# Seven block products instead of eight in the first feed-forward layer of the last four chunks

## The chip, the cores and the metric

The kernel runs on one core of a Trainium2 chip. The metric is the device time of one execution in microseconds. Engines are called as in the profile: PE (TensorE, matrix products), PEld (its weight loads), DVE (VectorE), ACT (ScalarE), POOL (GpSimd) and SP (the queue that issues DMAs).

## What is computed

Attention over 8 batches and 8 heads (512 local rows with a window of 32, 32 global rows), then per batch of 544 rows and 512 columns a Fourier mixing and a feed-forward block:

```python
x = attn_out.transpose(0, 2, 1, 3).reshape(8, 544, 512)
u = x + real(fft(fft(x, axis=1), axis=2))
un = (u - mean(u)) / sqrt(var(u) + 1e-6)            # per row
out = u + relu(un @ w_ch1) @ w_ch2                   # w_ch1 512 x 2048, w_ch2 2048 x 512
```

The change is in `un @ w_ch1` alone.

## The kernel before

Every operand of a matrix product is split into two float16 parts (hi and lo), and a product is three matmuls: hi·hi, hi·lo, lo·hi, summed in PSUM.

The rows go through the feed-forward block in 17 **chunks** of 256 rows. Chunks 2b and 2b+1 are rows of batch b, chunk 16 holds the 32 rows that each batch has left over. For a chunk, `l_bn` and `l_v` make mean and variance, `l_un` normalizes, `l_hi` (ACT) and `l_lo` (DVE) split, `l_turn` turns the result by a DMA transpose into the tile `uh`. Then there are 8 steps `fp`: `f_first` (L1047, 24 matmuls of 256 columns) makes 256 of the 2048 hidden columns for the 256 rows, `f_hi` (ACT, L1052) and `f_lo` (DVE, L1056) take relu and split, `f_second` (L1066, 12 matmuls of 512 columns) adds their share of the second layer to two accumulators in PSUM. `f_end` (L1071) scales and adds u, `f_out` (L1077, L1080) stores.

The order of work is made when the program is built. `Plan` is a list scheduler: each job has an engine, an estimated duration, dependencies, buffer rings and a target `t`; on every engine the ready job with the lowest target goes next. Jobs of the same function keep the order in which they were added (`j.prev`), so `f_end` of one chunk never goes behind that of a later chunk. What the scheduler decides is each engine's order. Its times are not kept on the chip: a `hold` delays a job in the plan, but on the chip the instruction runs as soon as what it waits for is done. Attention and the mixing (`d_...` functions) have low targets, the feed-forward matmuls have 10000 added to theirs, so they fill what PE has free. `targets` works targets backwards from successors that have one, and a job added with `back=False` gives none to those before it.

On PE, the attention of the last batch ends at about 821 us of the profile, its mixing at about 850 us, chunk 12 at about 855 us, and the rest is chunks 13 to 16, 42 us each.

POOL has the `lo` halves of attention, some sums of the mixing, and `l_root` (a few tiny instructions per chunk).

Of the kernel before, what the change touches and what calls it, by code (L numbers as in the profile page):

```python
# [14 lines left out]
AF = mybir.ActivationFunctionType  # L15
ALU = mybir.AluOpType
# [26 lines left out]
PEM, PEM0, SPM = 1.5, 0.6, 0.2  # L43
# [34 lines left out]
def shape_constants():  # L78
    a = np.arange
    t = 127 - a(P)[:, None]  # L80
    r = a(P)[:, None]
    k = np.concatenate([a(128, 0, -1), a(144, 272), [0], a(129, 144), [272], a(129, 144)])
    k = np.concatenate([k[0::2], k[1::2]])[None, :]
    tt = np.concatenate([[0], a(129, 144), [272], a(415, 400, -1)])[:, None]
    c1 = np.zeros((P, 2, 2, NK), np.float16)
    c1t = np.zeros((P, 2, NK), np.float16)
    c2 = np.zeros((P, 2, 2, 2, NH), np.float16)
    for i, fn in enumerate((np.cos, np.sin)):
        for j, v in enumerate(_hi_lo(fn(2 * np.pi * ((t + 1) * k % T) / T))):
# [24 lines left out]
class Job:
# [180 lines left out]
class Kern:  # L295
    def __init__(self, tc, stack, ins, out):
        self.tc, self.nc, self.out = tc, tc.nc, out
        nc = self.nc
        self.qk, self.vd, self.gd = ins["qk"], ins["v"], ins["g"]
        self.wd = (ins["moe_w_ch1"], ins["moe_w_ch2"])  # L300
        ep = lambda **k: stack.enter_context(tc.tile_pool(**k))
        c = self.cp = ep(name="cst", bufs=1)
        self.mskb = c.tile([P, 4, 256], U16, name="msk")
        self.msk = self.mskb.bitcast(BF16)
        self.consts = ins
        self.part = c.tile([P, P], F32, name="part")
# [4 lines left out]
        vN = c.tile([P, 2, 1300], F16, name="vN")  # L311
# [3 lines left out]
        self.vf = [c.tile([P, 5, 2, D], F32, name=f"vf{i}") for i in range(4)]  # L315
# [658 lines left out]

    def u_all(self, c):
        if c == 16:
            return self.u[16]
        return self.X[c // 2][:, (slice(1, 4, 2) if c % 2 else slice(0, 3, 2))]

    def u_row(self, c, j):  # L980
        return self.u_all(c)[:, j]

    def l_load(self):
        self.u[16] = u = self.p3.tile([P, 4, DM], F32, name="X")[:, 0:2]
        for j in range(2):
            self.nc.sync.dma_start(u[:, j], self.ul[j])

# [289 lines left out]
    def jobs_chunk(self, add, c):  # L1277
# [112 lines left out]
```

## Time and profile before

| | us |
|---|---|
| median of 3 runs | 1030.37 (1029.78 to 1032.76) |
| the profiled execution: its time | 1033.84 |
| its span, first to last instruction | 1032.1 |
| PE busy in the span | 929.6 (90%) |
| DVE, ACT, POOL busy | 658.1, 589.4, 531.8 |

The span is shorter than the execution's own time by 1.7 us, which lie around it. The profiled execution was 3.5 us slower than the median of the runs. Busy time counts overlapping matmuls once and does not say whether PE runs at its peak; for that one reads the distance between the starts of successive groups.

### The profile page before, as it was taken

The numbers are of one execution on the slowest core, as the hardware profiler recorded it, in microseconds if no ns is written. First come the engines' busy times: TensorE is split into PE (matmuls) and PEld (weight loads), VectorE is DVE, ScalarE is ACT, GpSimd is POOL, SyncE is SP. The second block draws the span as 40 slices with busy tenths as digits, with TensorE's granted clock in tenths as the row PEclk, the third lists the DMA queues.
The fourth block names the chain that finished last, engine by engine and source line by source line (L and its number), as shares of the span: only waits on it lengthen the run. The fifth ranks groups of instructions, "written<-read, shape, count | busy, mean of one in ns | idle before, by whom it ended". The sixth has DMA issues, their size and how long they took to land. (4 is left out here: it accounts for less than half of the span.)

```text
span 1032.1 us, 25192 instructions
## 1 busy us (share of the span) xinstructions
PE 929.6 (90%) x9864; PEld 651.0 (63%) x9864; DVE 658.1 (64%) x1773; ACT 589.4 (57%) x1291; POOL 531.8 (52%) x797
## 2 busy tenths in 40 slices
PE   2354459999999999999999999999999999999996
PEld 1243347767677767676766676777767676666673
DVE  4887999977768855785598568856775456311111
ACT  7996769973677477637863876487436332111110
POOL 7999756862687278626863774486437302000000
PEclk9985569999999999999999999999999999999998
DMA  9898356462685287328752864466225402102000
GB/s 364 254 269 238 105 107 138 106 140 42 141 130 133 45 160 154 77 55 147 134 131 53 132 155 96 88 117 140 39 55 102 83 1 64 42 1 41 2 21 21
DMA packets 221359, 111.52 MB, mean 108 GB/s; under 512 B 196376, under 2 KB 203704, under 8 KB 221240
## 3 DMA queue, kind: packets, MB, share of 16 engines
q1 hardware_dynamic: 221240, 109.91, 48.5%
q8 instruction: 77, 1.26, 0.5%
q14 instruction: 42, 0.34, 0.1%
HBM read 47.37 MB, written 9.44 MB: 55 GB/s over the span
## 5 line engine op out<-in xcount | busy, mean ns | idle before, releaser
L1047 PE MATMUL ps<-uh,wh 128*128 128x256 f16 x3264 | 379.7, 274 | 0.9 <-DMA uh<-unh 0.9
L1066 PE MATMUL acc<-wh,h 128*128 128x512 f16 x1632 | 375.2, 380 | 1.5 <-DVE h L1056 1.0
L1047 PEld LDWEIGHTS <-wh 128*128 128x128 f16 x3264 | 316.1, 98 | 51.2 <-issue 2.0
L1066 PEld LDWEIGHTS <-h 128*128 128x128 f16 x1632 | 154.3, 98 | 170.3 <-issue 2.5
L1056 DVE SCALAR_TENSOR_TENSOR h<-ps,h 128x512 f16<-128x512 f32 x136 | 93.6, 689 | 236.2 <-ACT h L1052 236.0
L1052 ACT ACTIVATE h<-ps 128x512 f16<-128x512 f32 x136 | 80.7, 593 | 256.4 <-PE ps L1047 255.8
L628 POOL TENSOR_TENSOR ph<-pe,ph 128x448 f16<-128x448 f32 (+1 forms) x128 | 139.4, 1103 | 79.3 <-ACT ph L623 63.3
L612 DVE CUSTOM_DVE_ANT_0 pe<-bk,msk,z 128x224 f32<-128x224 f32 (+1 forms) x256 | 102.4, 454 | 17.4 <-PE bk L604 14.2
L619 ACT ACTIVATE pe<-pe,nm 128x224 f32<-128x224 f32 (+1 forms) x256 | 104.7, 476 | 14.2 <-DVE nm L612 13.9
L1027 POOL TENSOR_TENSOR ve<-ve 128x2 f32<-128x2 f32 x17 | 3.9, 230 | 179.8 <-DVE un L1007 179.8
L649 PE MATMUL bk<-vN,pl 128*128 128x65 f16 x768 | 67.4, 201 | 26.6 <-DMA pl<-ph 17.9
L623 ACT ACTIVATE ph<-pe 128x448 f16<-128x448 f32 (+1 forms) x128 | 71.0, 579 | 22.0 <-DMA pl<-ph 15.2
L649 PEld LDWEIGHTS <-pl 128*128 128x128 f16 x768 | 59.5, 103 | 28.8 <-DMA pl<-ph 23.5
L652 PEld LDWEIGHTS <-pl 96*128 96x128 f16 (+1 forms) x768 | 57.5, 103 | 10.0 <-issue 5.9
L604 PE MATMUL bk<-kT,qT 64*128 64x192 f16 (+2 forms) x1536 | 57.5, 221 | 6.5 <-POOL kT L588 4.2
L604 PEld LDWEIGHTS <-qT 64*128 64x128 f16 x1536 | 50.1, 99 | 20.8 <-issue 16.7
L652 PE MATMUL bk<-vB,pl 96*128 96x65 f16 (+1 forms) x576 | 51.5, 202 | 0.0
L563 POOL TENSOR_TENSOR vN<-vf,vN 128x640 f16<-128x640 f32 x32 | 45.8, 1431 | 6.8 <-ACT vN L559 6.6
L419 PE MATMUL wl<-wm,partb 128*128 128x256 bf16 x64 | 18.8, 398 | 32.0 <-DVE wm L409 32.0
L588 POOL TENSOR_TENSOR kT<-qk,kT 128x559 f16<-128x559 f32 x32 | 40.7, 1271 | 11.8 <-ACT kT L583 11.6
L573 ACT ACTIVATE qk<-qk,z 128x559 f32<-128x559 f32 x64 | 43.7, 729 | 2.1 <-DVE z L514 2.0
L508 ACT ACTIVATE junk<-qk 128x512 f16<-128x512 f32 x64 | 41.3, 645 | 4.4 <-DMA qk<-in_qk 3.4
(170 smaller groups left out, 1350.0 us busy)
## 6 DMA issues: line engine op xcount, KB each, us to landing
qk<-in_qk SPq DMA_DIRECT2D x32, 535.5 KB, 5.2
rw<-in_moe_w_ch SPq DMA_DIRECT2D x22, 512.0 KB, 5.2
vf<-in_v SPq DMA_DIRECT2D x32, 320.0 KB, 3.3
out<-X SPq DMA_DIRECT2D x16, 512.0 KB, 3.1
raw<-in_moe_w_ch SPq DMA_DIRECT2D x10, 512.0 KB
vB<-vN SPq DMA_DIRECT2D x32, 97.5 KB, 2.2
vB<-vN SPq DMA_DIRECT2D x64, 32.5 KB, 2.0
pl<-ph SPq DMA_TRANSPOSE x128, 3.2
```

The costliest lines, as they stand in the source:

```text
L563: self.nc.gpsimd.tensor_sub(vN[:, :, 1, :, 0:64], self.st[p]["vf"], vN[:, :, 0, :, 0:64])
L604: nc.tensor.matmul(S[h][:, t + w0:t + w1], qT[r, a, j], kT[r, k0:k0 + w1 - w0], start=m == 0, stop=m == 2)
L612: nc.vector.tensor_tensor_reduce(self.per[j][:, h, 0:w], S[h][:, t:t + w], self.msk[:, j, 0:w], z[:, 8:9], 3e38, op0=ALU.add, op1=ALU.min, ...
L619: self.nc.scalar.activation(pe[:, h], pe[:, h], AF.Exp, bias=nm[:, h:h + 1], scale=-1.0)
L623: self.nc.scalar.activation(ph[:, 0, :, 0:WIDE[i % 4]], self.per[i % 4][:, :, 0:WIDE[i % 4]], AF.Copy)
L628: self.nc.gpsimd.tensor_sub(ph[:, 1, :, 0:w], self.per[i % 4][:, :, 0:w], ph[:, 0, :, 0:w])
L649: nc.tensor.matmul(pv[:, j % 2, h], pl[:, 4 * a + 2 * h], vN[:, j, c, h, :], start=m == 0, stop=False)
L652: nc.tensor.matmul(pv[:, j % 2, h], pl[0:n, 4 * a + 2 * h + 1], vb, start=False, stop=m == 2)
L1047: nc.tensor.matmul(ps[:, q], wt[:, w, c0:c0 + P], uh[:, :, 4 * a + kt, :], start=n == 0, stop=n == 11)
L1052: self.nc.scalar.activation(h[:, 0], self.fps[c, fp], AF.Relu)
L1056: self.nc.vector.scalar_tensor_tensor(h[:, 1], self.fps.pop((c, fp)), 0.0, h[:, 0], op0=ALU.max, op1=ALU.subtract)
L1066: nc.tensor.matmul(self.acc_f[c][j], h[:, a, q, j * P:(j + 1) * P], self.w[1, f][:, w, :], start=f == 0 and a == 0 and w == 0, stop=f == 1 ...
```

## The change

The last four chunks are done in two **pairs**, (13, 14) and (15, 16). For a pair the first layer is a product of 2 x 2 blocks: two halves of the 512 input columns, two chunks of rows, and for each `s` (0 to 7) two blocks of 128 hidden columns. It is done by Strassen's scheme in Winograd's form, with 7 block products P1 to P7 (each 6 matmuls of 256 columns: 2 for the block's 256 inputs, times 3 for hi and lo) instead of 8.

- **Sums of weights** (`t_sum`, `t_mix`, `t_lo` on POOL, `t_hi` on ACT), 8 times: two sums of hi and lo (512 columns each), four differences of 256, two splits. They lie in buffers of attention and start when its last results are there (`late`).
- **Sums of rows**: `s_pre` normalizes chunk A of a pair for P1 and P2; `s_un` normalizes both chunks, `s_mix` (4 DVE instructions of 256) makes the sums, `s_hi`, `s_lo`, `s_turn` split and turn four kinds of blocks (g = 0 to 3) for each of two row halves j. The split results go through a ring of two buffers (`unh`).
- **Phase one** of a pair: for each s, P1 and P2; their sum is relu'd, split and given to the second layer of chunk A (6 matmuls of 512 columns, `p_second` n = 0).
- **Phase two**: for each s, P4, P5, P6, P7, P3, seven small copies and sums (`p_copy` on ACT, `p_sum` on DVE), two splits, and the rest of the second layer: n = 2 (both blocks of chunk B, 12 matmuls), then n = 1 (chunk A, 6 matmuls).
- The mixing of the last batch gets its targets 40 us earlier (`BOOST`); `l_bn`, `l_v` of the four chunks give no targets backwards any more. `vf` and `pe`, four tiles each, become slices of one tile each.

```diff
+PAIRS = ((13, 14), (15, 16))
+PL = 45.0
+T_AT, T_PACE = 826.0, 7.5
+BOOST = 40.0
+PROD = {"P1": (0, 0, 0), "P2": (0, 2, 2), "P3": (2, 2, 3), "P4": (3, 0, 7), "P5": (1, 0, 4), "P6": (1, 2, 5), "P7": (2, 0, 6)}
...
+    def t_sum(self, n, o):
...
+        self.nc.gpsimd.tensor_add(f.rearrange("p a c -> p (a c)"), w[:, 0], w[:, 1])
+    def t_mix(self, n):
...
+        ve.tensor_sub(a[:, 0], f[:, 1], f[:, 0])
+        ve.tensor_sub(b[:, 0], g[:, 1], f[:, 1])
+        ve.tensor_sub(a[:, 1], g[:, 1], a[:, 0])
+        ve.tensor_sub(b[:, 1], a[:, 1], g[:, 0])
+    def t_hi(self, n):
...
+            self.nc.scalar.activation(t[:, 0, 2 * i:2 * i + 2], v, AF.Copy)
+    def t_lo(self, n):
...
+            self.nc.gpsimd.tensor_sub(t[:, 1, 2 * i:2 * i + 2], v, t[:, 0, 2 * i:2 * i + 2])
...
+    def s_mix(self, u, j):
...
+        ve.tensor_add(s[:, 0], b[:, 0], b[:, 1])
+        ve.tensor_sub(t[:, 0], a[:, 0], b[:, 0])
+        ve.tensor_sub(s[:, 1], s[:, 0], a[:, 0])
+        ve.tensor_sub(t[:, 1], a[:, 1], s[:, 1])
...
+    def p_mul(self, u, s, n):
...
+            for x, y in ((0, 0), (0, 1), (1, 0)):
+                nc.tensor.matmul(ps, w[x], a[:, :, k * y + o + kt, :], start=m == 0, stop=m == 5)
+                m += 1
...
+    def p_sum(self, u, s, o, a, b):
...
+        (ve.tensor_sub if o == "c21" else ve.tensor_add)(v[o], a, v[b])
+    def p_rest(self, u, s, n):
...
+        self.nc.vector.scalar_tensor_tensor(h[:, 1, q], v, 0.0, h[:, 0, q], op0=ALU.max, op1=ALU.subtract)
...
+    def jobs_mixes(self, add):
+        late = [("xM", 31), ("xgo", 7, 1)]
...
+                add("POOL", 1.16, self.t_sum, n, o, r=[self.whobj[0, 4 * (kt + 2 * o) + c], *late], w=[("qT", "T", n, o)], t=T, hold=T)
+            add("POOL", 2.6, self.t_mix, n, r=[("qT", "T", n, 0), ("qT", "T", n, 1)], w=[tw], t=T + 3)
+            add("ACT", 1.1, self.t_hi, n, r=[tw, *done.get(n, [])], w=[home], t=T + 5)
+            add("POOL", 2.4, self.t_lo, n, r=[tw, home], w=[home], t=T + 7)
+    def jobs_duo(self, add, u):
...
+        first = [*end, ("ht", 7), ("uh", 12)] if u == 0 else []
...
+                add("DVE", .58, self.s_un, u, j, n, r=[("uj", c, j), ("ve", c), *first], w=[un[n]], k=[("X", c // 2)], t=L, back=False)
...
+        for s in range(8):
+            b = prod(s, "P1", t)
+            b = prod(s, "P2", t)
+            summ(s, "c11", "P2", "x1", [b, x1, *end], [c11], own)
+            split(s, 0, .36, [c11], [], ("h", "s", u, s, 0), [f], t + STEP / 2 + 1)
+        for s in range(8):
...
+            b = prod(s, "P6", t)
+            summ(s, "x1", "P6", "x1", [b, x1], [x1], xk)
+            b = prod(s, "P7", t)
+            summ(s, "u3", "P7", "x1", [b, x1], [u3, ("xu", u, s)], xk)
+            summ(s, "c12", "x1", "c22", [x1, cz], [c12], [R, *xk], .34)
+            b = prod(s, "P3", t)
+            summ(s, "c21", "u3", "c21", [u3, cw], [cw], [R, ("xu", u, s)], .34)
+            summ(s, "c22", "u3", "c22", [u3, cz], [cz], [R, ("xu", u, s)], .34)
+            split(s, 2, .58, [cw, cz], [R], ("pl", "s", u, s), [f, f + 2], t + 1.5 * STEP + 2)
+            summ(s, "c12", "P3", "c12", [b, c12], [c12], [R])
+            split(s, 1, .36, [c12], [R], ("h", "s", u, s, 1), [f + 2], t + 1.5 * STEP + 1)
+        for n, c in enumerate(PAIRS[u]):
+            for j in range(2):
+                add("DVE", .72, self.f_end, c, j, r=[accs[n][j], ("ve", c), ("uj", c, j)], w=[("uj", c, j)], k=[("X", c // 2)], t=-1e3, back=False)
+            add("SP", .39, self.f_out, c, r=[("uj", c, 0), ("uj", c, 1)], w=[("out", c)], k=[("X", c // 2)], svc=3.2, t=T, back=False)
...
         for c in range(17):
-            self.jobs_chunk(add, c)
+            if c not in MATE:
+                self.jobs_chunk(add, c)
+        self.jobs_mixes(add)
+        for u in range(len(PAIRS)):
+            self.jobs_duo(add, u)
         plan.targets(1.3)
+        for j in plan.jobs:
+            if j.fn.__name__.startswith("d") and j.a[0] == B - 1:
+                j.t -= BOOST
```

## Rows read from the trace of the kernel before

**Rows 1.** The page: busy share of PE and the granted clock of PE in 40 equal slices of the span (tenths).

```profile
PE   2354459999999999999999999999999999999996
PEclk9985569999999999999999999999999999999998
```

**Rows 2.** Waits of PE between 150 us and the end: the longest in total: who waited for whom, total us, times, longest us.

```profile
PE bk L649 <- DMA pl<-ph: 4.2, 4, 2.6
```

**Rows 3.** The first-layer matmuls between 855 and 1023 us: count, busy us and mean ns, idle us before them.

```profile
L1047 PE MATMUL ps<-uh,wh 128*128 128x256 f16 x768 | 88.4, 273 | 0.0
```

**Rows 4.** Timeline of the tail of the kernel, steady part: start us, duration us, engine, line, operation.

```profile
993.46 2.78 PE L1047 MATMUL ps<-uh,wh 128*128 128x256 f16 x24
996.08 2.75 PE L1066 MATMUL acc<-wh,h 128*128 128x512 f16 x12
996.28 0.60 ACT L1052 ACTIVATE h<-ps 128x512 f16<-128x512 f32 x1 [4.61 <-PE ps L1047]
996.91 0.69 DVE L1056 SCALAR_TENSOR_TENSOR h<-ps,h 128x512 f16<-128x512 f32 x1 [4.52 <-ACT h L1052]
998.67 2.78 PE L1047 MATMUL ps<-uh,wh 128*128 128x256 f16 x24
```

**Rows 5.** Timeline of the last matmuls and the end of the kernel.

```profile
1016.92 5.34 PE L1066 MATMUL acc<-wh,h 128*128 128x512 f16 x24
...
1021.09 0.75 DVE L1071 SCALAR_TENSOR_TENSOR X<-acc,ve,X 128x512 f32<-128x512 f32 x1 [2.64 <-PE acc L1066]
1021.87 1.82 SPq L1080 DMA_DIRECT2D out<-X  x2
1022.30 0.75 DVE L1071 SCALAR_TENSOR_TENSOR X<-acc,ve,X 128x512 f32<-128x512 f32 x1 [0.47 <-PE acc L1066]
```

**Rows 6.** Timeline around the end of the last batch's mixing and of chunk 12.

```profile
831.97 0.75 DVE L847 SCALAR_TENSOR_TENSOR eh<-s,dsc,eh 128x512 f16<-128x512 f32 x1
...
836.76 0.35 PE L893 MATMUL bk<-c1r,eh 128*128 128x144 f16 x3
...
849.40 1.65 DVE L945 SCALAR_TENSOR_TENSOR X<-bk,dsc,X 128x256 f32<-128x256 f32 x4
...
850.19 5.35 PE L1066 MATMUL acc<-wh,h 128*128 128x512 f16 x24
...
853.30 0.55 DVE L1007 TENSOR_SCALAR un<-X,ve 128x512 f32<-128x512 f32 x1
...
855.33 1.40 DVE L1071 SCALAR_TENSOR_TENSOR X<-acc,ve,X 128x512 f32<-128x512 f32 x2
855.38 5.40 PE L1047 MATMUL ps<-uh,wh 128*128 128x256 f16 x48
```

**Rows 7.** DMA issues between 800 and 900 us: count and median us from issue to landing.

```profile
uh<-unh SPq DMA_TRANSPOSE x6, 4.4
```

**Rows 8.** Groups of instructions over the whole span, shapes apart: count, busy us and mean ns, idle us before them.

```profile
L665 DVE TENSOR_TENSOR X<-bk,dn 128x256 f32<-128x256 f32 x64 | 27.2, 424 | 2.2
L1015 DVE TENSOR_TENSOR unh<-un,unh 128x512 f16<-128x512 f32 x34 | 23.8, 699 | 1.4 <-ACT unh L1011 1.2
L588 POOL TENSOR_TENSOR qT<-qk,qT 128x512 f16<-128x512 f32 x32 | 38.6, 1207 | 0.0
L552 POOL TENSOR_TENSOR gn<-gn,ge 128x256 f32<-128x256 f32 x8 | 5.5, 683 | 0.0
```

**Rows 9.** The same view for four DVE sums whose two inputs lie both in SBUF.

```profile
L826 DVE TENSOR_TENSOR e<-e 128x256 f32<-128x256 f32 x8 | 7.5, 938 | 0.0
L802 DVE TENSOR_TENSOR s<-s 128x256 f32<-128x256 f32 x8 | 5.7, 709 | 0.0
L803 DVE TENSOR_TENSOR s<-s 128x128 f32<-128x128 f32 x8 | 5.1, 642 | 0.3
L834 DVE TENSOR_TENSOR s<-s 128x256 f32<-128x256 f32 x8 | 4.3, 542 | 0.3
```

**Rows 10.** Single lines: shortest, median and longest ns of those four, and of one that reads PSUM (L665).

```profile
L826 DVE TENSOR_TENSOR e<-e x8: 416/966/1572, 117.4 to 826.0; 128x256 f32<-128x256 f32 x8
L802 DVE TENSOR_TENSOR s<-s x8: 411/418/1470, 120.6 to 827.2; 128x256 f32<-128x256 f32 x8
L803 DVE TENSOR_TENSOR s<-s x8: 291/292/1327, 122.0 to 827.6; 128x128 f32<-128x128 f32 x8
L834 DVE TENSOR_TENSOR s<-s x8: 424/425/1358, 123.3 to 828.2; 128x256 f32<-128x256 f32 x8
L665 DVE TENSOR_TENSOR X<-bk,dn x64: 424/424/426, 52.4 to 821.7; 128x256 f32<-128x256 f32 x64
```

**Rows 11.** Timeline of DVE and POOL at 691 us.

```profile
690.77 2.17 POOL L628 TENSOR_TENSOR ph<-pe,ph 128x448 f16<-128x448 f32 x2 [0.26 <-POOL xt L761]
691.04 1.01 DVE L817 TENSOR_TENSOR e<-e 128x128 f32<-128x128 f32 x1
691.97 1.12 DVE L818 TENSOR_TENSOR e<-e 128x128 f32<-128x128 f32 x1
```

**Rows 12.** Stretches of time: length, then busy us (and instructions) of PE, PEld, DVE, ACT, POOL, the granted clock of PE, DMA share, GB/s.

```profile
150.00:154.00 4.00, 4.00 (x54) 3.08 (x53) 2.61 (x8) 0.99 (x3) 3.08 (x12) 0.74 0.91 175
...
1025.00:1026.00 1.00, 0.00 (x0) 0.00 (x0) 0.00 (x0) 0.00 (x0) 0.00 (x0) 0.94 0.25 74
1026.00:1027.00 1.00, 0.00 (x0) 0.00 (x0) 0.00 (x0) 0.00 (x0) 0.00 (x0) 0.50 0.26 102
```

More of the change, by code (lines that the diff above doesn't have):

```diff
@@ L54 @@
 BLOCK = (0, 3, 1, 2)
+PAIRS = ((13, 14), (15, 16))
+MATE = {c: (u, n) for u, v in enumerate(PAIRS) for n, c in enumerate(v)}
+APER = 109.0
+PL = 45.0
+T_AT, T_PACE = 826.0, 7.5
+BOOST = 40.0
 def _hi_lo(c):
@@ L310, in __init__ @@
         self.kT = [c.tile([P, 1152], F16, name=f"kT{i}") for i in range(NKB)]
[L311 removed]
+        vN = self.vna = c.tile([P, 2, 1300], F16, name="vN")
         self.vN = [vN[:, i].rearrange("p (j a h d) -> p j a h d", j=5, a=2, h=2) for i in range(2)]
@@ L314, in __init__ @@
         self.vB = [v.rearrange("p (j a h d) -> p j a h d", j=3, a=2, h=2) for v in self.vBf]
-        self.vf = [c.tile([P, 5, 2, D], F32, name=f"vf{i}") for i in range(4)]
+        self.vfa = c.tile([P, 4, 5, 2, D], F32, name="vf")
+        self.vf = [self.vfa[:, i] for i in range(4)]
         self.junk = c.tile([P, 640], F16, name="junk")
@@ L320, in __init__ @@
             nc.gpsimd.memset(self.accx[i], 2.0 ** -90)
-        ph = c.tile([P, 3, 1024], F16, name="ph")
+        ph = self.pha = c.tile([P, 3, 1024], F16, name="ph")
         self.phr = [ph[:, i].rearrange("p (a h c) -> p a h c", a=2, h=2) for i in range(3)]
-        self.per = [c.tile([P, 2, 256], F32, name=f"pe{i}") for i in range(4)]
+        self.pea = c.tile([P, 4, 2, 256], F32, name="pe")
+        self.per = [self.pea[:, i] for i in range(4)]
         self.xd = c.tile([P, DM], F32, name="xd")
@@ L983, in l_load @@
     def l_load(self):
-        self.u[16] = u = self.p3.tile([P, 4, DM], F32, name="X")[:, 0:2]
+        u = self.x8()[:, 0:2]
         for j in range(2):
@@ new lines, in t_hi, with s_un @@
+    def t_hi(self, n):
+        self.tm[n] = t = self.t_home(n)
+        for i, v in enumerate(self.tw[n]):
+            self.nc.scalar.activation(t[:, 0, 2 * i:2 * i + 2], v, AF.Copy)
+    def t_lo(self, n):
+        t = self.tm[n]
+        for i, v in enumerate(self.tw.pop(n)):
+            self.nc.gpsimd.tensor_sub(t[:, 1, 2 * i:2 * i + 2], v, t[:, 0, 2 * i:2 * i + 2])
+    def s_un(self, u, j, n):
+        c = PAIRS[u][n]
+        self.L[c]["un", j] = un = self.p1.tile([P, DM], F32, name="un", tag=("un", "lw")[n])
+        self.nc.vector.tensor_scalar(un, self.u_row(c, j), self.L[c]["ve"][:, 1, j:j + 1], self.L[c]["ve"][:, 2, j:j + 1], op0=ALU.mult, op1=ALU.add)
@@ new lines, in s_lo, with s_turn, x8 @@
+    def s_lo(self, u, j, g):
+        hl = self.tf[u, j, g]
+        self.nc.vector.tensor_sub(hl[:, 1], self.s_val(u, j, g), hl[:, 0])
+    def s_turn(self, u, j, g):
+        hl = self.tf.pop((u, j, g))
+        if j == 0:
+            self.ug[u, g] = self.s_home(u, g)
+        self.nc.sync.dma_start_transpose(self.ug[u, g][:, j], hl.rearrange("p a d -> p (a d)"))
+    def x8(self):
+        if 16 not in self.u:
+            self.u[16] = self.p3.tile([P, 4, DM], F32, name="X")
+        return self.u[16]
@@ new lines, in s_home @@
+    def s_home(self, u, g):
+        if g == 0:
+            return self.p2.tile([P, 2, 8, P], F16, name="uh", tag="uh")
+        if g == 3:
+            return self.wb.tile([P, 2, 4, P], F16, name="ug", tag=f"w{12 + u}")
+        if u == 0:
+            v = self.pea[:, 2 * g - 2:2 * g].bitcast(F16)
+            return v.rearrange("p j h (k n) -> p j (h k) n", n=P)
+        if g == 1:
+            return self.p1.tile([P, 2, 8, P], F16, name="ug", tag="eh")
+        return self.X[6][:, 0:3:2].bitcast(F16).rearrange("p j (k n) -> p j k n", n=P)
@@ new lines, in p_mul @@
+    def p_mul(self, u, s, n):
+        nc, (c, q) = self.nc, divmod(s, 2)
+        g, o, src = PROD[n]
+        x = n == "P1" and u == 0
+        ps = (self.psa.tile([P, 512], F32, name="ps1") if x else self.bank(("bank", n, u, s)))[:, 0:256]
+        self.pb[u, s, n], a = ps, self.ug[u, g]
+        k = a.shape[2] // 2
+        m = 0
+        for kt in range(2):
+            if src < 4:
+                i, h = divmod(src, 2)
+                w = self.w[0, 4 * (kt + 2 * i) + c]
+                w = [w[:, x, 256 * h + P * q:256 * h + P * q + P] for x in range(2)]
+            else:
+                t = self.tm[2 * c + kt]
+                w = [t[:, x, src - 4, P * q:P * q + P] for x in range(2)]
+            for x, y in ((0, 0), (0, 1), (1, 0)):
+                nc.tensor.matmul(ps, w[x], a[:, :, k * y + o + kt, :], start=m == 0, stop=m == 5)
+                m += 1
@@ new lines, in p_keep @@
+    def p_keep(self, s):
+        if s < 2:
+            return self.mskb.bitcast(F32).rearrange("p a c -> p (a c)")[:, 256 * s:256 * s + 256]
+        if s == 2:
+            return self.vna.rearrange("p a c -> p (a c)")[:, 2048:2560].bitcast(F32)
+        if s < 5:
+            return self.xd[:, 256 * s - 768:256 * s - 512]
+        n, o = divmod(s - 5, 2)
+        if (n, "k") not in self.tw:
+            self.tw[n, "k"] = self.p1.tile([P, 2, 256], F32, name="xk", tag=f"z{n}")
+        return self.tw[n, "k"][:, o]
@@ new lines, in p_sum, with p_part, p_relu @@
+    def p_sum(self, u, s, o, a, b):
+        ve, v = self.nc.vector, self.p_bufs(s)
+        a = self.pb[u, s, a] if a in PROD else v[a]
+        (ve.tensor_sub if o == "c21" else ve.tensor_add)(v[o], a, v[b])
+    def p_part(self, s, n):
+        v = self.p_bufs(s)
+        return (v["c11"], v["c12"], v["r"][:, 1:3])[n], (0, 1, slice(0, 2))[n]
+    def p_relu(self, u, s, n):
+        if n == 2:
+            h = self.p3.tile([P, 2, 2, 256], F16, name="hb", tag="pl")
+        else:
+            h = self.p2.tile([P, 2, 2, 256], F16, name="h", bufs=3)
+        self.hp[u, s, n] = h
+        v, q = self.p_part(s, n)
+        self.nc.scalar.activation(h[:, 0, q], v, AF.Relu)
@@ new lines, in p_rest, with p_second, second @@
+    def p_rest(self, u, s, n):
+        h = self.hp[u, s, n]
+        v, q = self.p_part(s, n)
+        self.nc.vector.scalar_tensor_tensor(h[:, 1, q], v, 0.0, h[:, 0, q], op0=ALU.max, op1=ALU.subtract)
+    def p_second(self, u, s, n):
+        f = s // 2 * 4 + s % 2
+        self.second(u, n // 2, self.hp.pop((u, s, n)), ((f, 0),) if n == 0 else ((f + 2, 1),) if n == 1 else ((f, 0), (f + 2, 1)), n != 1 and s == 0, n > 0 and s == 7)
+    def second(self, u, n, h, fs, first, last):
+        nc, c = self.nc, PAIRS[u][n]
+        if first:
+            self.acc_f[c] = [self.psa.tile([P, DM], F32, name="ps1") if n else self.ps.tile([P, DM], F32, name=f"acc{j}") for j in range(2)]
+        for j in range(2):
+            for f, q in fs:
+                for a, w in ((0, 0), (0, 1), (1, 0)):
+                    nc.tensor.matmul(self.acc_f[c][j], h[:, a, q, j * P:(j + 1) * P], self.w[1, f][:, w, :],
+                                     start=first and q + a + w == 0, stop=last and q == 1 and a == 1)
```

126 lines of the change are left out of this document (123 added, 3 removed).

## Prediction

> **What bounds the kernel now.** I read the page first: from the seventh slice of 40 on PE is busy nine tenths or more at a full granted clock [rows 1]. Busy is not peak, so the waits come next: over 880 us PE waits a few microseconds, most of it in four waits for a turned softmax block [rows 2]. Then the distances. In the tail a step of 24 matmuls of 256 columns lasts from 993.46 to 996.08 us, 2.62 us or 109 ns a matmul; the 12 matmuls of 512 columns last to 998.67, 2.59 us or 216 ns each [rows 4]. There is no gap between the two kinds, and none before any of the 768 first-layer matmuls behind 855 us [rows 3]. So in the stretch that the change rewrites, matmuls set the time one for one, and a matmul saved counts whole as long as PE is never left waiting. ACT and DVE need 0.60 and 0.69 us per step there [rows 4] and idle for the rest. The end hangs on the last accumulator: matmuls end at 1022.26 us, the second `f_end` at 1023.05, the span at 1032.1 [rows 5].
>
> **What is saved.** Four chunks take 768 first-layer matmuls [rows 3]; two pairs of 8 steps with 7 products of 6 matmuls take 672. 96 fewer at 109 ns [rows 4] are 10.5 us. The second layer keeps its count (per step 6 + 12 + 6 matmuls of 512 columns, as for two chunks before). Smaller groups cost nothing by themselves, since the change from one kind to the other is free today [rows 3, 4].
>
> **What is added on other engines.** Phase one of a step is 12 × 0.109 + 6 × 0.216 = 2.6 us of PE, against one DVE sum and one DVE split of about 0.42 us each (a 256-column sum takes 0.42, [rows 8]). Phase two is 30 × 0.109 + 18 × 0.216 = 7.2 us, against eight DVE instructions of 0.42 or 0.7 us, 3.6 us in all. The chain behind P7 is four sums, a relu (0.60) and a split (0.69), 3.0 us; the next step's products and the previous step's 18 second-layer matmuls (3.9 us) lie beside it. All this is at nothing while that cover holds; without it each step would lose some tenths. I take 0.5 us for it, with 0 and 2 as ends. Merging `vf` and `pe` into one tile each is at nothing: the scheduler's objects and the slices read are the same, and `ph` and `vN` are already sliced so. The earlier targets for the last batch's mixing I also put at nothing: on PE it went ahead of every feed-forward job already.
>
> **The end.** `p_second` n = 1 (chunk A) comes behind n = 2 (chunk B), so chunk 16 is summed first, but `f_end` and `f_out` keep the order of adding, chunk 15 first. The four `f_end` run back to back at 0.65 to 0.75 us [rows 5, 6]; the last, of chunk 16, ends about 2.1 us behind the last matmul instead of 0.8, and chunk 15's store is now ahead of chunk 16's in SP's queue and on the DMA engines. That is 1.3 us at least, 2.7 if the store's data delays the other's by its whole length (about 1.4); I take 1.9 longer.
>
> **The rows for phase two.** This is the term that decides. P4 to P7 need blocks of chunk 14, a chunk of the last batch. Its rows are done at 851.05 us, and its `l_un` runs at 853.30 [rows 6]; `s_un` and `s_mix` can't be earlier unless the mixing is. From there DVE has 4 normalizations (0.55), 8 sums (0.42) and 6 splits (0.7, or 0.42 for the two narrow ones), 9.1 us. Ahead of them in its queue go the `f_end` pair of chunk 12 (1.4) and the sums and splits of some six steps of phase one (5.0). That gives 868.8 for the last split, and 873.2 with the landing of a turn, 4.4 us [rows 7]. The ring of two buffers gives about the same: three rounds of split and landing behind 855 us. SP's queue holds only these turns, chunk 12's store and the left-over rows then. PE reaches P7 of the first step at 855.2 [rows 6] + 8 × 2.6 + 3 × 0.66 = 878.0. With 1.3 us for a somewhat later mixing there are 3.5 us to spare.
>
> But POOL now works all this while. The sums of weights may start with the last attention results at about 822 us; the hold of 826 is only in the plan. Each of the eight rounds is 4 instructions of 512 columns (1.21) and 4 of 256 (0.68), 7.6 us [rows 8], and about 1.3 us for `t_hi` (two of 0.60): 8 rounds fill 822 to 892. At 691 us two DVE sums of 128 columns took 1.01 and 1.12 us while POOL ran two instructions [rows 11], where 0.29 is the shortest [rows 10]. Sums that read PSUM never vary (424 to 426 ns). So DVE instructions with both inputs in SBUF and POOL's wait for each other. Over four such lines the mean lies above the shortest by 0.52, 0.30, 0.35 and 0.12, mean 0.32 us [rows 9, 10], with POOL busy about half the time. Of the new DVE work 18 instructions for the rows and about 6 splits of phase one are of this kind: 24 × 0.32 = 7.7 us, less 3.5 to spare: PE idles 4.2 us in all around the start of phase two. The ends are 0 (no waiting), and 24 × 0.78 = 18.7 less 3.5, 15 us, if each waits as at 691 us. I take the mean because it is over 32 instances, though POOL will be busier than it was for them. The first mixing sums of the last batch meet POOL too, but the matmuls that need them (836.76) start 4 us behind the last split's start (831.97) [rows 6].
>
> The Trainium skill says the same in "GPSIMD Engine Reference", Key points: GpSimd shares its SBUF interfaces with VectorE, and instructions with two SBUF inputs contend. The trace agrees (1.01 and 1.12 us against 0.29). By the engine times without it nothing would be lost here, and the sum would be 1022.3.
>
> **Sum.** −10.5 + 1.9 + 4.2 + 0.5 = −3.9 us. The profiled execution took 1033.84, so its like would take 1029.9. It lies 3.5 us above the median of the runs; against the median 1030.37 the forecast is **1026.5**.
>
> **Rivals.**
> - *The rows are in time.* Stall under 1.5 us, as when the mixing ends earlier or POOL waits long for `t_hi`, which ACT's queue may hold up. For it: 3.5 us to spare before contention. Time 1030.4 − 10.5 + 1.9 + 0 to 2 = 1022 to 1024. Chance 0.23.
> - *Slower: the stall is long.* Same place, each DVE instruction waiting most of a POOL instruction. It gives back the saving when PE idles 8.1 us in all, that is at 0.48 us a wait, between the mean and the rows at 691 us. For it: POOL without pauses. Against it: the mean. Also PE's clock: behind the last matmul (1022.26) it is granted 0.94 of a slice from 1025, then 0.50 from 1026, which is 1.2 GHz, and in the slice in which PE became busy throughout again it was 0.74 [rows 12], so about 1 us of 4 lost. A long idle stretch adds 1 to 2 us. Time 1029.5 (7 us idle) to 1040; chance 0.26, of it 0.09 within 3.1 us of before.
> - *The sums of weights are late.* P5 of steps 6 and 7 needs rounds 6 and 7, at 878 + 6 × 7.2 = 921 us; uncontended they are there at 892. DVE has some 70 instructions of the kind in between; at 0.32 they push POOL to about 915, at 0.5 to 927. Then 5 to 8 us on top of the forecast, 1031 to 1035; chance 0.09.
>
> "TensorE: Matmul & The Clock Gate" of the Trainium skill, "Why this matters for your kernels", warns of idle gaps between bursts of matmuls, behind which the clock is back at half. The last slices agree (0.50); if the wait comes in one piece, the slower rival gains by it, and if it is spread over the steps of phase one, it does not.
>
> **How the numbers follow.** The forecast's own case is a stall of 1.5 to 7 us, 1023.5 to 1029.5, chance 0.42. 0.3% or 3.1 us is about what this measurement tells from no change, so faster means below 1027.3: 0.23 and two thirds of the forecast's case, 0.52. Same is the rest of that case and 0.09 of the long stall: 0.22. Slower is the rest, 0.26. The range leaves out the shortest tail with no stall at all, and the upper part of the long stall: 1021 to 1037.
>
> **What the profile after would show.** 672 matmuls of 256 columns in the pairs, still 109 ns apart; waits of PE between 850 and 885 us for turned rows or for DVE's splits, 4 us in sum; DVE sums in SBUF of 0.4 to 1.5 us between 822 and 900, with POOL filled; about 11.7 us from the last matmul to the end instead of 9.8. The prediction is wrong if attention or the mixing of the last batch ends many microseconds earlier or later, since each shifts the rows against PE one for one; if POOL or ACT's order makes DVE wait more or less than 0.32; or if phase two's chain is longer than its cover.

## Result and the profile after

The changed kernel takes 1039.97 us, median of 4 (1038.62 to 1041.4); before, on the same chip, 1030.74. The ratio is 1.0087, 95% interval 1.0067 to 1.0108: **slower by 0.9%**. The profiled executions span 1039.6 us (after) and 1032.1 (before). The forecast was 1026.5, faster.

Functions that both kernels have stand 12 lines further down in the changed one. Waits of TensorE (PE) between 854 and 950 us, the stretch of the first pair (who waits, for whom, total us, times, longest):

```profile
PE bk L1207 <- ACT ph L1229: 4.1, 3, 2.6
PE bk L1207 <- DMA pe<-unh: 2.1, 1, 2.1
PE ps L1265 <- DVE hb L1252: 1.2, 1, 1.2
PE acc L1265 <- ACT h L1247: 1.0, 1, 1.0
PE bk L1207 <- DVE ph L1234: 1.0, 2, 0.6
PE acc L1265 <- DVE h L1252: 0.5, 1, 0.5
```

Before, no first-layer matmul waited in this stretch [rows 3]. Now PE waits 9.9 us, and only 2.1 of them for turned rows (`pe<-unh`); the rest is for phase two's own chain: copies (L1229), sums (L1234), relu (L1247) and splits (L1252).

Stretches of the same trace: length, then busy us (and instructions) of PE, PEld, DVE, ACT, POOL, granted clock, DMA share, GB/s:

```profile
850.00:925.00 75.00, 64.93 (x400) 40.43 (x399) 69.32 (x126) 25.19 (x59) 62.29 (x94) 0.93 0.25 49
...
876.00:880.00 4.00, 2.97 (x18) 1.69 (x19) 3.08 (x5) 1.55 (x4) 4.00 (x4) 1.00 0.35 66
880.00:884.00 4.00, 2.06 (x11) 1.54 (x11) 3.39 (x7) 0.78 (x2) 3.92 (x6) 0.77 0.75 196
884.00:888.00 4.00, 3.17 (x16) 2.08 (x15) 2.96 (x4) 1.66 (x4) 4.00 (x4) 0.50 0.03 7
...
882.00:889.00 7.00, 6.17 (x30) 4.26 (x30) 5.50 (x7) 2.44 (x5) 6.92 (x8) 0.51 0.35 94
909.00:913.00 4.00, 3.24 (x11) 1.62 (x11) 3.94 (x5) 1.59 (x4) 3.92 (x5) 0.57 0.00 0
...
949.00:1027.00 78.00, 78.00 (x529) 51.66 (x528) 34.89 (x84) 19.82 (x48) 0.00 (x0) 1.00 0.04 14
```

In 850 to 925 us DVE is busy 69.3 of 75 us and POOL 62.3; PE is idle 10.1 us. Behind the wait of 2.1 us the clock is granted at 0.77 and then 0.50, which is 1.2 GHz, so a PE that reads as busy does half the work. It is low twice, at 882 to 889 us (0.51) and at 909 to 913 us (0.57), which is about 5 us of full clock lost. In pair 2, 949 to 1027 us, POOL has stopped and PE is never idle.

From the first product (854.50) to the start of the last matmul (1027.3) are 172.8 us. The matmuls alone need 2 × (336 × 0.109 + 192 × 0.216) = 156.2 us; 16.6 us are lost, all in pair 1: 10.1 idle, about 5 at the lower clock, and a rest of about 1.5 that is neither (1.6 in the run with the hold below, whose clock stays at 1.00 in the pairs). With −10.5 saved, an end 2.1 us longer and a start 0.7 us earlier (the first product follows chunk 12 at 854.5 instead of 855.2) the sum is +7.5 us, and so much the spans differ. The medians differ by 9.2, with 6.9 to 11.1 as the interval.

Why phase two's chain got long is seen on single lines (shortest, median and longest ns; start of the first and last):

```profile
L1234 DVE TENSOR_TENSOR ph<-kT,ph x32: 418/419/1376, 887.8 to 1020.3; 128x256 f32<-128x256 f32 x32
...
L1234 DVE TENSOR_TENSOR ph<-bk,ph x16: 411/419/421, 890.0 to 1020.7; 128x256 f32<-128x256 f32 x16
...
L1134 DVE TENSOR_SCALAR un<-X,ve x8: 534/544/1380, 836.7 to 917.9; 128x512 f32<-128x512 f32 x8
...
L1013 DVE SCALAR_TENSOR_TENSOR ve<-mv,ve x17: 160/161/642, 136.9 to 903.9; 128x2 f32<-128x2 f32 x17
...
L1108 POOL TENSOR_TENSOR tf<-wh x16: 1141/1151/1368, 817.0 to 902.7; 128x512 f32<-128x512 f16 x16
```

The first two are the same line and size. With both inputs in SBUF the sum takes up to 1376 ns, with one in PSUM (`bk`) never over 421. The longest excess, 0.96 us, is within one POOL instruction (1.15). POOL waits as well: the same subtraction of 256 columns takes it 0.72 to 1.17 us.

```profile
L1117 POOL TENSOR_TENSOR pgr<-tf,pgr x8: 716/905/1167, 821.0 to 911.7; 128x256 f32<-128x256 f32 x8
```

How such an excess reaches PE, timeline at 907 us:

```profile
907.37 0.61 ACT L1124 ACTIVATE tp<-vf 128x512 f16<-128x512 f32 x1
907.54 1.17 POOL L1129 TENSOR_TENSOR tp<-pgr,tp 128x512 f16<-128x512 f32 x1 [3.66 <-ACT tp L1124]
907.61 1.38 DVE L1134 TENSOR_SCALAR un<-X,ve 128x512 f32<-128x512 f32 x1
908.67 1.33 POOL L1129 TENSOR_TENSOR tp<-vf,tp 128x512 f16<-128x512 f32 x1
909.02 0.42 ACT L1161 ACTIVATE unh<-un 128x256 f16<-128x256 f32 x1 [1.04 <-DVE un L1134]
909.02 1.26 DVE L1141 TENSOR_TENSOR et<-un 128x256 f32<-128x256 f32 x1
909.35 0.64 ACT L1229 ACTIVATE ph<-bk 128x256 f32<-128x256 f32 x2
...
909.76 1.44 PE L1207 MATMUL bk<-pe,wh 128*128 128x256 f16 x6 [2.59 <-ACT ph L1229]
```

A row of pair 2 (`un`, L1134) meets POOL and takes 1.38 us instead of 0.54. ACT has its upper half (L1161) next in its queue and waits; behind it stand the copies of P4 and P5 (L1229), ready before, and PE waits 2.59 us for them. Two upper halves of weight sums (L1124) stand ahead of the row on ACT, until 907.98, so the row accounts for about 1.5 us of this wait.

### The profile page after: what moved, and what is told of

Same layout as the page of the kernel before. It is cut to its first block, busy times and chain, and to the rows that moved or that the text cites. A ratio compares the mean times of both kernels' runs of the same rounds, so it can differ in the third digit from the quotient of the medians.

```text
span 1039.6 us, 25360 instructions
## 1 busy us (share of the span) xinstructions
PE 922.8 (89%) x9768; PEld 640.7 (62%) x9768; DVE 734.4 (71%) x1929; ACT 621.6 (60%) x1379; POOL 599.8 (58%) x861
## 4 chain that ended last, share of the span: by engine, by line
PE 61%; DVE 7%; DMA 4%; POOL 4%; ACT 3%; issue 1%; SPq 1%; DVEq 0%; POOLq 0%; ACTq 0%
PE ps L1059 20%; PE acc L1078 20%; PE bk L1207 4%; PE ps L1265 3%; PE bk L616 3%; PE acc L1265 2%; DMA pl<-ph 2%; PE bk L940 2%; PE bk L661 1%; PE bk L664 1%; DMA X<-xt 1%; PE bk L905 1%; PE bk L688 1%; PE bk L724 1%; DVE ph L1234 1%
## 5 line engine op out<-in xcount | busy, mean ns | idle before, releaser
L1059 PE MATMUL ps<-uh,wh 128*128 128x256 f16 x2496 | 290.3, 273 | 3.5 <-DVE h L1068 2.7
L1078 PE MATMUL acc<-wh,h 128*128 128x512 f16 x1248 | 286.5, 379 | 1.9 <-DVE h L1068 1.1
L1059 PEld LDWEIGHTS <-wh 128*128 128x128 f16 x2496 | 240.2, 98 | 38.7 <-issue 4.7
L1078 PEld LDWEIGHTS <-h 128*128 128x128 f16 x1248 | 116.3, 98 | 131.0 <-DVE h L1068 2.9
L1068 DVE SCALAR_TENSOR_TENSOR h<-ps,h 128x512 f16<-128x512 f32 x104 | 71.5, 688 | 117.2 <-ACT h L1064 117.0
L1064 ACT ACTIVATE h<-ps 128x512 f16<-128x512 f32 x104 | 61.5, 592 | 117.6 <-PE ps L1059 116.9
L1265 PE MATMUL acc<-wh,h 128*128 128x512 f16 x192 | 46.6, 379 | 1.6 <-ACT h L1247 1.0
L575 POOL TENSOR_TENSOR vN<-vf,vN 128x640 f16<-128x640 f32 x32 | 44.5, 1393 | 4.3 <-ACT vN L571 4.0
L1265 PE MATMUL ps<-wh,hb 128*128 128x512 f16 x192 | 45.2, 385 | 1.2 <-DVE hb L1252 1.2
```

Source lines behind the costliest of these rows:

```text
L1059: nc.tensor.matmul(ps[:, q], wt[:, w, c0:c0 + P], uh[:, :, 4 * a + kt, :], start=n == 0, stop=n == 11)
L1064: self.nc.scalar.activation(h[:, 0], self.fps[c, fp], AF.Relu)
L1068: self.nc.vector.scalar_tensor_tensor(h[:, 1], self.fps.pop((c, fp)), 0.0, h[:, 0], op0=ALU.max, op1=ALU.subtract)
L1078: nc.tensor.matmul(self.acc_f[c][j], h[:, a, q, j * P:(j + 1) * P], self.w[1, f][:, w, :], start=f == 0 and a == 0 and w == 0, stop=f == 1 ...
L1265: nc.tensor.matmul(self.acc_f[c][j], h[:, a, q, j * P:(j + 1) * P], self.w[1, f][:, w, :], start=first and q + a + w == 0, stop=last and q ...
```

## Experiments

Theory A: DVE instructions that meet POOL's weight sums wait them out, and that stretches phase two of pair 1. Theory B: the rows of pair 2, queued between phase two's instructions on DVE and ACT, do it. Two more stand in the expectations: C, the lower clock alone does it; D, phase two is too tight by itself.

**Without the sums.** Each of POOL's instructions on 2 columns of 256; the lower half of the summed weights is not used.

```
-        self.nc.gpsimd.tensor_add(f..., w[:, 0], w[:, 1])
+        v = w.rearrange("p x (a c) -> p x a c", a=2)
+        self.nc.gpsimd.tensor_add(f[:, :, 0:2], v[:, 0, :, 0:2], v[:, 1, :, 0:2])
...
-            w = [t[:, x, src - 4, ...] for x in range(2)]
+            w = [t[:, 0, src - 4, ...] for x in range(2)]
```

> The sums of weights and their lower halves are made on 2 of the 256 columns of each block only, and the products of the summed blocks take the upper half twice: GpSimd has almost nothing to do between 820 and 920 us, every other instruction stays in its place and length. Theory A (GpSimd's sums and VectorE's instructions with two SBUF inputs hold each other up, and phase two of the first pair is stretched by that): pair 1 takes about 80 us on PE instead of 94.9, the time falls by 12 to 16 us to 1024 to 1028. Theory B (the rows of pair 2, queued between the sums of pair 1's phase two, delay them): no more than 3 us are gained, 1037 to 1040. Theory C (half clock alone after short gaps): as B, since the gaps stay.

Ratio 0.9933 (0.9905 to 0.9961). The pairs take 157.5 us, 1.3 above the matmuls; one wait is left, 1.2 us for turned rows. The SBUF line of phase two in this run, two of its sums on the timeline of DVE, then the same two in the changed kernel:

```profile
L1236 DVE TENSOR_TENSOR ph<-kT,ph x32: 414/418/420, 882.2 to 1006.7; 128x256 f32<-128x256 f32 x32
```

```profile
882.25 0.75 DVE L1236 TENSOR_TENSOR ph<-kT,ph 128x256 f32<-128x256 f32 x2
```

```profile
887.81 2.25 DVE L1234 TENSOR_TENSOR ph<-kT,ph 128x256 f32<-128x256 f32 x2
```

Two sums in 0.75 us against 2.25. POOL's work is the root. C falls as a cause by itself: 10.1 of the 16.6 us lost are idle time, and with the waits gone the clock stays at 1.00 in both pairs. D falls, since phase two has the same instructions here and its one wait is for turned rows.

**Rows of pair 2 held back.**

```
-  add("DVE", .58, self.s_pre, u, j, ..., t=L0, back=False)
+  add("DVE", .58, self.s_pre, u, j, ..., t=L0, back=False, hold=905.0 * u)
...
-  add("DVE", .58, self.s_un, u, j, n, ..., t=L, back=False)
+  add("DVE", .58, self.s_un, u, j, n, ..., t=L, back=False, hold=916.0 * u)
```

> The rows of pair 2 are prepared only when pair 1's phase two is nearly through (in the plan from 905 us for the first block and from 916 us for the rest, instead of 870 and 887). Theory B expects pair 1 to lose 5 us less or better, a time of 1032 to 1035. Theory A expects little, 1037 to 1041: VectorE has some 20 instructions of two SBUF inputs less beside GpSimd's sums, but GpSimd is still there for the chain.

Ratio 1.0026 (1.0002 to 1.005): theory B's number, 6.3 us less lost (166.5 us for the pairs). But PE's idle time in 850 to 925 us fell only from 10.1 to 8.7 us; what went is mostly the lower clock. A stretch with a pause as long as in the changed kernel kept the full clock:

```profile
872.00:876.00 4.00, 2.97 (x18) 1.69 (x19) 3.06 (x5) 1.57 (x4) 4.00 (x4) 1.00 0.34 66
876.00:880.00 4.00, 1.47 (x12) 1.17 (x12) 2.92 (x7) 0.82 (x2) 3.92 (x6) 1.00 0.78 197
880.00:884.00 4.00, 2.78 (x24) 2.34 (x24) 3.26 (x4) 1.30 (x4) 4.00 (x4) 1.00 0.02 4
```

**Both edits.** Sums on 2 columns and rows held.

> Both pairs, the sums on 2 columns of 256 as in the run without sums, and pair 2's rows held as in the run with the hold. If the rows of pair 2 hurt only because GpSimd stretches them and the chain (A is the root, B the way), the hold gains nothing more here: within 1.5 us of the run without sums, 1022 to 1026. If the two add up, it falls by about 6 us more, which is below what the matmul counts allow (1030.7 - 10.5 + 2.2 = 1022.4), so it would stop there.

Ratio 0.9928 (0.9912 to 0.9944), pairs 157.4 us. Without sums the hold is worth nothing: A is the root, B one way by which it reaches PE.

**Copies for sums.** Does a GpSimd instruction with one SBUF input hold DVE up as well?

```
-        self.nc.gpsimd.tensor_add(f..., w[:, 0], w[:, 1])
+        self.nc.gpsimd.tensor_copy(f..., w[:, 0])
...
-        ve.tensor_sub(a[:, 0], f[:, 1], f[:, 0])
+        ve.tensor_copy(a[:, 0], f[:, 1])
...
```

> Each sum of GpSimd for the weights is a copy of one of its inputs of the same size (one SBUF input instead of two), in the same place and number. If it is the second input stream that shuts out VectorE, the time falls as without sums, to about 1024 to 1028, with GpSimd still filled. If any GpSimd work on SBUF does it, it stays in proportion to GpSimd's busy time, 1033 to 1039.

Ratio 0.9938 (0.9916 to 0.9961), but the question is not answered: the copies are shorter (0.70 us in the mean instead of 1.19 for 512 columns), so POOL is busy 36.7 of 60 us in 860 to 920, not 50.4. DVE does still wait:

```profile
L1234 DVE TENSOR_TENSOR ph<-kT,ph x32: 415/419/827, 883.6 to 1008.1; 128x256 f32<-128x256 f32 x32
```

So two more runs, one with sums on 160 columns and one with every copy made twice:

> Both pairs, every sum of GpSimd made on 160 of the 256 columns (the products of the summed blocks take the upper half twice), so that GpSimd is busy about as long as with the copies, but with two SBUF inputs each time. If it is GpSimd's busy time that counts, the result is that of the copies, 0.992 to 0.996 of before. If the second input stream counts by itself, it stays slower than the copies at the same busy time, 0.998 to 1.004.

> As the run with copies, but every copy of a sum or a mix is made twice (of both inputs in turn), so that GpSimd is filled between 860 and 920 us about as with the sums (50 us of 60 busy) and still reads one SBUF input at a time. If it is GpSimd's busy time that shuts out VectorE, with one input or two, PE loses 8 us or more in the two pairs, 1.001 to 1.010 of before. If the second input stream counts, it stays near the single copies, 0.993 to 0.998.

0.9987 (0.9965 to 1.0008) with 160 columns, the number expected if the second input counts, but POOL was busy 44.5 us, longer than with the copies (36.7), so the run does not tell the two apart. 1.0001 (0.9985 to 1.0017) with the copies twice, POOL busy 50.8 us: between the two expected ranges. Doubling the copies costs 0.6%, so one input is enough to shut DVE out. At equal busy time copies (7.1 us lost) still cost less than sums (16.6); some 5 us of that difference are clock. Whether the second input counts by itself stays open.

**Shorter instructions.** Every sum in two of half the columns.

```
-        ve.tensor_sub(a[:, 0], f[:, 1], f[:, 0])
...
+        for k in (slice(0, 128), slice(128, 256)):
+            ve.tensor_sub(a[:, 0, k], f[:, 1, k], f[:, 0, k])
...
```

> The changed kernel with each GpSimd sum cut into two of half the columns: the same sums, about the same GpSimd time in all (a little more), but no instruction longer than about 0.7 us. If a VectorE instruction waits out the one GpSimd instruction that it meets, so that the length of one counts, the longest VectorE sum of two SBUF inputs falls from 1.38 to about 0.9 us and the time to 0.998 to 1.004 of before. If only GpSimd's total time counts, it stays at 1.007 or above, with the same lost time in pair 1.

1.0089 (1.0067 to 1.011). The first half of the expectation held, the second not; the line as above, then the stretch from 860 to 920 us:

```profile
L1237 DVE TENSOR_TENSOR ph<-kT,ph x32: 418/419/897, 886.6 to 1018.8; 128x256 f32<-128x256 f32 x32
```

```profile
860.00:920.00 60.00, 48.06 (x294) 30.15 (x293) 50.02 (x97) 20.79 (x47) 55.75 (x106) 0.91 0.23 47
```

The longest single wait is shorter, but POOL is busy 55.8 of 60 us, and as much is lost. This trace also showed a second queue: ACT, asked for the upper half of a weight sum (`t_hi`), waits for POOL's mix with phase two's copies behind it (in brackets: idle us and for what):

```profile
882.97 0.63 ACT L1126 ACTIVATE vf<-pgr 128x512 f16<-128x512 f32 x1 [7.12 <-POOL pgr L1119]
...
884.04 0.61 ACT L1164 ACTIVATE unh<-un 128x512 f16<-128x512 f32 x1
884.56 0.36 ACT L1232 ACTIVATE ph<-bk 128x256 f32<-128x256 f32 x1
...
884.98 1.44 PE L1210 MATMUL bk<-ug,tq 128*128 128x256 f16 x6 [3.63 <-ACT ph L1232]
```

In the changed kernel ACT waits so too, 5.43 us before 882.98. Theory E: ACT's queue is a way of its own.

**Upper halves later, and upper halves on GpSimd.**

```
-            add("POOL", 2.6, self.t_mix, n, ...)
+            add("POOL", 5.0, self.t_mix, n, ...)
```

```
-            self.nc.scalar.activation(t[:, 0, 2 * i:2 * i + 2], v, AF.Copy)
+            self.nc.gpsimd.tensor_copy(t[:, 0, 2 * i:2 * i + 2], v)
...
-            add("ACT", 1.1, self.t_hi, n, ...)
+            add("POOL", 1.5, self.t_hi, n, ...)
```

> The changed kernel, the plan alone told that a mix takes GpSimd 5.0 us instead of 2.6 (beside VectorE the four subtractions took 3.4, and the queue before them runs late), so that ScalarE gets the upper halves of the weight sums later in its order and doesn't stand in front of phase two's copies waiting for GpSimd. Theory E (ScalarE's queue is a second way by which GpSimd's lateness reaches TensorE): ScalarE's waits for GpSimd in 860 to 890 us, 8.4 us in the changed kernel, fall under 3 us, pair 1 loses 3 us less or better, 1.002 to 1.006 of before. Theory A alone (VectorE is the only way): 1.007 to 1.010.

> The changed kernel, the upper halves of the weight sums made by GpSimd itself by copies: ScalarE never waits for GpSimd there, but GpSimd has about 12 us more work beside VectorE. Theory E: in spite of that, 1.000 to 1.006 of before. Theory A alone: more GpSimd time means more waiting of VectorE, 1.009 or above.

1.0069 (1.0047 to 1.0091) and 1.0144 (1.0112 to 1.0175). In the first, ACT's waits for POOL fell to 2.2 us as meant, but PE is idle 11.1 us in 850 to 925 all the same: the waits are now for DVE's sums (3.5 us) as well as for the copies (3.4). In the second no ACT instruction waits for POOL in 860 to 925, and it is the slowest of all: 1.9 us more are lost in the pairs, and PE waits 3.9 us for DVE in the mixing of the last batch, which it does not do in the changed kernel. Theory E falls as a cause by itself; more GpSimd time beside DVE costs more, whoever waits for it.

**The end.** `f_end` and `f_out` of the second chunk of a pair ahead of the first's.

```
-        for n, c in enumerate(PAIRS[u]):
+        for n, c in reversed(list(enumerate(PAIRS[u]))):
             for j in range(2):
                 add("DVE", .72, self.f_end, c, j, ...)
```

> The results of the second chunk of a pair, whose sums are complete first, are also finished and stored first. Only the end changes: from the last matmul to the end about 9.5 us instead of 12.05, so 2 to 3 us below the changed kernel, 1036.5 to 1038. All theories on pair 1 expect its 94.9 us unchanged.

1.0061 (1.0043 to 1.0079), 0.26% or 2.7 us under the changed kernel's ratio, as expected. The two intervals overlap; that the end is shorter is seen in the next two traces.

**Both pairs, order alone.** Rows held and the end order; then with the longer planned mix too.

> Both pairs with the full sums, pair 2's rows held, and the second chunk finished first: the gains of these two edits alone (6 and 2.6 us against the changed kernel) should add, since one lies in pair 1 and the other at the end: 0.998 to 1.002 of before, no faster than before. If it comes out at 0.996 or lower, two pairs with the hold are as good as one pair.

> Both pairs with full sums, with three edits to the order together: the longer planned mix, pair 2's rows held, the second chunk finished first. Without the first it was 0.9989 of before. Theory E: 0.994 to 0.997. Theory A alone: 0.998 to 1.000, as without the longer planned mix.

0.9989 (0.9972 to 1.0005), then 0.9953 (0.9935 to 0.997). In the first the last matmul ends at 1020.75 us and the span 9.5 us behind it, instead of 11.9 in the changed kernel and 9.8 before. In the second the longer planned mix, worth little alone, gives 0.36%: pairs 162.4 us instead of 166.5. Theory E had expected that (0.994 to 0.997): once DVE's queue is relieved, ACT's does count. Its waits for POOL in 860 to 950 us fall from 11.9 to 2.2 us.

**One pair.** `PAIRS = ((15, 16),)`, chunks 13 and 14 as before.

> Only chunks 15 and 16 are a pair, 13 and 14 are done as before; the sums of weights run beside chunks 13 and 14, where the VectorE instructions between two matmul groups read PSUM. Theory A: nothing is lost anywhere, half the saving (5.2 us) less the longer end (2.2 us): 3 us below before, 1027 to 1029. Theory B: the same, since no second pair's rows are in the way. If phase two is too tight by itself (theory D, no cover for its chain), it loses some microseconds here too: 1031 to 1036.

1.0017 (1.0001 to 1.0034), median 1034.0 us. That is theory D's time and not that of A and B, but not D's place: the pair takes 77.9 us without a wait. Two waits of ordinary chunks, 4.2 us, were new. The timeline around the longer:

```profile
879.32 0.83 DVE L1141 TENSOR_TENSOR et<-un 128x256 f32<-128x256 f32 x1
...
880.08 0.94 DVE L1142 TENSOR_TENSOR pg<-un 128x256 f32<-128x256 f32 x1
...
880.53 0.60 ACT L1064 ACTIVATE h<-ps 128x512 f16<-128x512 f32 x1 [4.61 <-PE ps L1059]
...
880.95 0.95 DVE L1143 TENSOR_TENSOR et<-et,un 128x256 f32<-128x256 f32 x1
...
881.93 1.25 DVE L1144 TENSOR_TENSOR pg<-un,et 128x256 f32<-128x256 f32 x1
883.11 0.68 DVE L1068 SCALAR_TENSOR_TENSOR h<-ps,h 128x512 f16<-128x512 f32 x1
...
883.84 3.67 PE L1078 MATMUL acc<-wh,h 128*128 128x512 f16 x10 [2.98 <-DVE h L1068]
```

The split L1068 reads PSUM and takes its usual 0.68 us, but stands behind the four sums of `s_mix`, which take 3.9 us beside POOL. I had looked at what an instruction itself waits for and not at what it is queued behind. Two steps take this away: the rows prepared behind the sums (`l_bn` of chunks 15 and 16 with `hold=905.0`) with the end order; then the sums behind chunk 14's rows (`T_AT` 853 instead of 826, the hold at 910).

> One pair as in the run with chunks 15 and 16 alone, but the preparation of its rows (from the statistics on) starts in the plan at 905 us, behind the last sums of weights, and the second chunk is finished and stored first. Theory A+B (a VectorE instruction with two SBUF inputs beside GpSimd's sums takes about twice its length, and what is queued behind it on VectorE reaches TensorE late): the two waits of TensorE for the split of the hidden layer, 4.2 us in that run, fall to about 1.2 us, and with the shorter end (2 to 3 us) the time is 0.3 to 0.7% below before, 1024 to 1028. If the pair costs something that has nothing to do with GpSimd's sums, it stays at or above before.

> One pair with the end order and the held rows, and the sums of weights start only when chunk 14's rows are prepared (about 853 us in the plan instead of 826), so that no row preparation at all lies beside them until their last two rounds. If the remaining wait of 1.2 us in the run before came from that meeting, it goes, and the time falls by 1 to 2 us more against before: ratio 0.995 to 0.997, 1025.5 to 1028. If it stays, something else makes it.

0.9972 (0.9959 to 0.9985), a little less gain than expected, one wait of 1.2 us left; then 0.9937 (0.9916 to 0.9959), **faster than before by 0.6%**, with none:

```profile
850.00:925.00 75.00, 75.00 (x515) 50.23 (x514) 29.51 (x57) 19.06 (x34) 61.14 (x76) 1.00 0.11 30
```

POOL is as busy as in the changed kernel (61 us), but DVE only 29.5 instead of 69.3.

**The runs with both pairs**, from their traces (that with the end order alone left none that shows this): first product to the last matmul's start, what is above 156.2, PE idle in 850 to 925, POOL busy in 860 to 920 (us).

| kernel | ratio | pairs | lost | idle | POOL |
|---|---|---|---|---|---|
| both edits | 0.9928 | 157.4 | 1.2 | 1.2 | 15.5 |
| without sums | 0.9933 | 157.5 | 1.3 | 1.2 | 23.8 |
| copies | 0.9938 | 159.3 | 3.1 | 2.4 | 36.7 |
| order, three edits | 0.9953 | 162.4 | 6.2 | 5.0 | 48.1 |
| 160 columns | 0.9987 | 162.8 | 6.6 | 4.3 | 44.5 |
| hold, end order | 0.9989 | 166.5 | 10.3 | 8.7 | 46.8 |
| copies twice | 1.0001 | 163.3 | 7.1 | 5.9 | 50.8 |
| hold | 1.0026 | 166.5 | 10.3 | 8.7 | 45.2 |
| longer planned mix | 1.0069 | 172.4 | 16.2 | 11.1 | 42.5 |
| changed kernel | 1.0087 | 172.8 | 16.6 | 10.1 | 50.4 |
| sums split | 1.0089 | 173.9 | 17.7 | 11.9 | 55.8 |
| upper halves on GpSimd | 1.0144 | 174.7 | 18.5 | 13.2 | 52.4 |

With the order as it is, the loss grows with POOL's time from the run without sums over the copies, the 160 columns and the changed kernel to the split sums; the copies made twice lie below this row. Edits to the order move the loss at about the same POOL time. POOL's time holds its own waits for DVE, so it is not a pure measure of the work that POOL was given.

## Why the prediction was wrong

- **The saving, right.** 96 fewer matmuls at 109 ns: pair 2 takes 77.9 us from its first product to the start of its last matmul, where 336 × 0.109 + 192 × 0.216 is 78.1.
- **The end, right.** 11.9 us from the last matmul's end to the end of the span instead of 9.8 [rows 5]: +2.1, put at +1.9; and its cause is the order of `f_end` and `f_out`, since with that turned it is 9.5.
- **Earlier work, right.** The first product starts at 854.5 us, where chunk 13 started at 855.2 before, and PE is never idle in the 35.0 us from the last attention result (819.46) to it. No cost of merging buffers and of the earlier mixing is seen. In the other runs with both pairs this start lies between 850.5 and 860.8 us, so a cost of a microsecond would not show.
- **"The rows for phase two", +4.2: right in its mechanism, wrong in its place.** PE waits 2.1 us for turned rows at 881.94. The forecast counted 24 DVE instructions that meet POOL, all ahead of phase two's first products, the ones that stood before a date. The mean excess was well guessed: `ph<-kT` takes 701 ns in the mean over 858 to 930 us, 0.28 above its shortest, where 0.32 was put.
- **"All this is at nothing while that cover holds", +0.5: this is the step that failed.** Phase two's five DVE instructions per step with two SBUF inputs, and the rows of pair 2 queued between them, were costed at their lengths without POOL, although the prediction itself let POOL work until 892 us or later, through the first steps of phase two, and named a chain longer than its cover among the signs of being wrong. DVE is then busy 69.3 us of 75, its waits for POOL included, and has no room to make up; sums, copies and splits arrive late, with 7.8 of the 9.9 us of waiting. The terms 4.2 and 0.5 stand against 16.6.
- **The clock, too small.** The slower rival gave it 1 to 2 us; it took about 5.
- **Sums late (0.09), no.** They run until 921 us, but PE is never found waiting for one in the changed kernel.
- The slower rival's time (1029.5 to 1040) held 1039.97, but by luck: its condition, 0.48 us a wait or more in one place, was not met (0.28). There were more waits and not longer ones, spread over pair 1, and the instructions queued behind them.

The Trainium skill says in "SBUF — State Buffer", section "SBUF: two separate sides", that a VectorE instruction with two SBUF inputs and a GpSimd instruction that reads SBUF take their shared ports for a whole instruction each, and the one that comes second blocks fully. The runs agree: the longest excess of the same DVE sum is 0.96 us beside sums of 1.15 (median), 0.48 when these are cut to 0.67, 0.41 beside copies of 0.62, and none without.

## What to carry to other kernels

Before giving GpSimd new work, list every VectorE instruction that runs during all of it, not only those ahead of the next date, and add what is queued behind them on VectorE and ScalarE, PSUM readers included. Where both can't be apart in time, take the smaller change: one pair whose rows and weight sums never meet gave 0.6%, two pairs with everything at once lost 0.9%. Order edits alone brought the two pairs to within the noise of the one pair (0.9953 and 0.9937). Order was worth as much as arithmetic: three edits to the order alone turned the two pairs from 1.0087 to 0.9953.

## What was not expected of the hardware

- A DVE instruction with one tensor input also waits for POOL: `un<-X,ve` took 534 ns at its shortest and 1380 at its longest (535 to 547 in the run without sums), and even one of two columns (`ve<-mv,ve`, two inputs) 160 and 642.
- A GpSimd copy, with one SBUF input, shuts DVE out as a sum does: up to 827 ns for a sum of 415.
- Shorter GpSimd instructions shorten the single wait (the longest sum from 1376 to 897 ns) and not the loss.
- The wait goes both ways: a GpSimd subtraction of 0.72 us took up to 1.17.
- The clock fell to 0.50 in the changed kernel behind 876 to 884 us, 3.0 of 8 us idle, and stayed at 1.00 with the rows held behind 872 to 880, 3.6 of 8 us idle. What decides between them the runs don't show.
